# The state's factor from one sum of three angles, and a new set of planner numbers

## The chip, the cores and the metric

One core of a Trainium2 chip runs the program. The metric is the device time of one execution in microseconds, the median of several. Times inside an execution come from the hardware profiler and count from the span's first instruction.

## The reference, cut to what matters

```python
# attention: a recurrence with a complex decay a = a_re + i a_im per (token, row of the state)
mag = np.sqrt(a_re * a_re + a_im * a_im)
scale = np.minimum(mag, 0.999) / (mag + 1e-06)
a_re_n, a_im_n = a_re * scale, a_im * scale
for t in range(S):                                  # B, H, S, D = 4, 8, 768, 48
    new_re = ar * S_re - ai * S_im
    new_im = ar * S_im + ai * S_re
    S_re, S_im = new_re + einsum(k[t], v[t]), new_im
    y[t] = einsum(q[t], S_re)
# then x = y as rows (3072 x 384): experts of 384 tokens each (relu(x @ w1) @ w2),
# and last (x @ w_a) * (x @ w_b) @ w_out
```

## The kernel before

The attention works in chunks of 128 tokens. Its loop index i runs over 12 pairs: six chunks, each with two halves of the batch, so that pair i covers two units (n = 2i and 2i + 1) of 128 tokens by 8 heads by 48. For each pair `gates` makes the logarithm of the decay's size, `e`, and its angle, `th`, per token, on ScalarE (Ln, Exp, Square, Arctan) and VectorE. `sums` sums both over the chunk's tokens, from the middle outwards, by matmuls with constant triangles (`Ws`, `Wt`, L354). The sum of the sizes goes through two exponentials into `ea`; the sum of the angles, in turns, is reduced to within half a turn by VectorE and is then `r` (L389, L391). `turned` takes two sines of `r`: `s2` = 2 sin(pi r) squared (L409, L411), which is 1 - cos, and `sn` = sin(2 pi r) (L410); with them it turns q and k into `nat` (L413 to L422). `unit` transposes `nat` (L519), copies it (`qkT`, L522), makes the scores (L531), masks them (`Ab`, L533), multiplies with v (L559), adds the state's part (L566), and sends the rows out (L572 to L586). `outer` (L542) and `keep` (L549) make the chunk's addition to the state, `xs`.

`factor(i)` runs for i from 2 to 11, ten times. It carries the state from pair i - 2 over to pair i: the state has to be multiplied, per head and row of the state, by a complex factor that spans from the middle of one chunk to the middle of the next. Its angle has three parts: what the earlier chunk sums to behind its middle (row 127 of pair i - 2), the angle `th` of the new chunk's first token, and what the new chunk sums to ahead of its middle (row 0 of pair i). These are single rows of 16 x 48 values; small DMAs on SP's queue bring them into the tile `fw` (16 partitions): L427 from `turned`, L342 from `gates`. Before, the rows were of `s2` and `sn` for the first and third part, and ScalarE took the cosine and the sine of `th` (L450, L452). VectorE then multiplied the three complex numbers out (`one`, L456 to L460; `two`, L464 to L467) and the factor's size in (`three`, L471 to L476). TensorE transposes the result (L482), ScalarE copies it to `pb` (L485), VectorE multiplies `xs` with it (L492, `rta` and `rtb`), one SP DMA pair swaps halves (L496), and VectorE adds to the state `Sb` (L500), which L566 reads.

All of this is recorded as tasks with an engine, an estimated duration, reads and writes. `Plan.order` is a list scheduler over these estimates: at each step it takes the engine on which something can start first, and among the tasks of that engine that could start at that time the one of lowest rank, rank = due x STRETCH - tail + EARLIER[kind], where due is PERIOD x (i + 1) or near it and the kind is the engine's letter with the written tile's name (P TensorE, V VectorE, A ScalarE, S SP, G GpSimd; `Sqk` are the loads of q and k, `Sre` those of a_re, `Vft` VectorE's factor work). A task never starts before its inputs and its buffer are free; nearly every tile has one or two buffers. ScalarE has two tables of functions: "E" with Ln and Exp, "T" with Arctan and Sin. A task whose table isn't loaded gets SWITCH added to its rank, and cannot start before PATIENCE us after it is ready unless the waiting tasks of its table add up to ENOUGH us. The instructions are then issued in that order on each engine's queue, so each queue waits in order. The planner doesn't know POOL's set-up work, which is ahead of it on POOL's queue.

After the attention come the router, which counts tokens per expert, and the experts with their last layer; these are 780 us of mostly TensorE work, written out in another way.

Of the kernel before, what the change touches and what calls it, by code (L numbers as in the profile page):

```python
# [14 lines left out]
AF = mybir.ActivationFunctionType  # L15
OP = mybir.AluOpType
# [5 lines left out]
B, H, S, D = 4, 8, 768, 48  # L22
# [4 lines left out]
LN = math.log  # L27
HALF_PI = math.pi / 2
TB = 12
MAGIC = 1.5 * 2 ** 21  # L30
TURN = 1.5 * 2 ** 23
LIFT = 12.125
PERIOD = 22.0
SWITCH = 13.0
HOP = {"P": 0.22, "V": 0.08, "A": 0.08, "S": 0.08, "G": 0.08}
NPAIR = 2
LANDING = 1.5
SPLIT_PAIRS = 3
EARLIER = {'Acc': 8, 'Aea': 5, 'Ag': -6, 'Aln': -14, 'Apb': -15, 'AqkT': -2, 'Arec': -6, 'As2': 2, 'Asf': -23, 'Asn': 6, 'Ath': 6, 'Axo': 6, 'AyT': 17, 'G-': 1, 'PF': -10, 'PHH': -10, 'PLL': -2, 'PO': -10, 'PS': 13, 'PTT': -1, 'PX': 2, 'PY': 5, 'Sends': 9, 'Sfw': 6, 'Sim': 10, 'Sqk': 11, 'Sre': -1, 'Ssw': 15, 'Sv': -13, 'V-': -5, 'VAb': 3, 'VS': 3, 'Ve': 10, 'Vearly': -1, 'Veb': 2, 'Vft': 21, 'Vg': 4, 'Vlg': -17, 'Vn4': -5, 'Vnat': -7, 'Vr': 4, 'Vrt1': -2, 'Vsetup': -4, 'Vxs': 4}
STRETCH = 0.844334  # L40
LONG = ("LL", "HH")
ENGINES = "PVASG"
SLOW = 1.03
SINGLE = 1
PATIENCE = 9.0
ENOUGH = 8.5
BUFS = {'rho': 2, 'ln': 2, 'g': 2, 'e': 2, 'ea': 2}


# [4 lines left out]
class Plan:  # L54
# [31 lines left out]
    def order(self):  # L86
# [5 lines left out]
        for t in reversed(T):  # L92
            own = [T[u]["tail"] for u in users[t["n"]] if T[u]["due"] == t["due"]]
            t["tail"] = t["dur"] + t["land"] + HOP[t["eng"]] + max(own, default=0.0)
            t["rank"] = t["due"] * STRETCH - t["tail"] + EARLIER.get(t["kind"], 0.0)
        left = [len(t["after"]) for t in T]
# [10 lines left out]
        def places(key):  # L107

            if len(key[0]) == 2:
                if key[0] in LONG:  # L110
                    used = [h for k, h in holds.items() if k[0] in LONG]
                    if len(used) >= SPLIT_PAIRS:
                        return []
# [3 lines left out]
        while any(waiting.values()):  # L117
            best = None
            for e, w in waiting.items():
# [14 lines left out]
                if not ok:  # L134
                    continue
                first = min(ok)[0]
                now = [(T[n]["rank"] + (SWITCH if T[n]["table"] and T[n]["table"] != table else 0.0), n)
                       for at, n in ok if at <= first + 1e-9]
# [50 lines left out]
def attention(tc, q, k, v, a_re, a_im, wg, x_dram, consts, L, guard, router, tail_work=None):  # L189
# [4 lines left out]
    A, V, G, PE = nc.scalar, nc.vector, nc.gpsimd, nc.tensor  # L194
    SP = nc.sync
    NB = NU // 2
    PI = math.pi
    with ExitStack() as st:
# [5 lines left out]
        def many(pool, n, shape, name, dt=F32):  # L204
            return [pool.tile(shape, dt, name=f"{name}{i}") for i in range(n)]

        W1, W2 = 2 * HD, HD
        plan = Plan(many(ps, NPAIR, [128, 2, 512], "pair") + many(ps, 8 - 2 * NPAIR, [128, 512], "bank"))
# [3 lines left out]
        tables = {"E": "natural_log_exp_and_others", "T": "trig_and_small"}  # L212
        A.preload_act_table_set(tables["E"])
        bias = {}
        for nm, x in (("one", 1.0), ("shift", LIFT), ("tiny", LN(2.0e-6)), ("quarter", HALF_PI)):
            bias[nm] = cst.tile([128, 1], F32, name="b_" + nm)
            V.memset(bias[nm], x)

# [34 lines left out]
        ends = cst.tile([2 * H, NB, 2, D], F32, name="ends")  # L253
        fw = many(cst, 4, [2 * H, 8, D], "fw")
# [139 lines left out]
        def turned(i, due):  # L394

            a = dict(due=due)
            c, pair = divmod(i, 2)
            j = i % 2
            (r, kr), (s2, ks2), (sn, ksn), (ea, kea), (eb, keb) = [buf(nm, i) for nm in ("r", "s2", "sn", "ea", "eb")]
            ea, eb = [t.rearrange("p (a r d) -> p a r d", a=2, d=D) for t in (ea, eb)]  # L400
            y = i % len(nat)

            def both(k):
                return [k + (0,), k + (1,)]
            for us in parts(i):
                def K(k, us=us):
                    return [k + (u,) for u in us]
                x, z = cols(us), rows_of(us)
                plan.add("A", took(0.83, us), lambda x=x: A.activation(s2[:, x], r[:, x], AF.Sin, scale=PI), K(kr), K(ks2), table="T", **a)  # L409
                plan.add("A", took(0.83, us), lambda x=x: A.activation(sn[:, x], r[:, x], AF.Sin, scale=2 * PI), K(kr), K(ksn), table="T", **a)  # L410
                plan.add("A", took(0.83, us), lambda x=x: A.activation(s2[:, x], s2[:, x], AF.Square, scale=math.sqrt(2.0)),  # L411
                         K(ks2), K(ks2), **a)
                plan.add("V", took(1.7, us), lambda z=z: V.tensor_mul(eb[:, :, z], ea[:, :, z], ld_qk[j][:, :, z]),  # L413
                         K(kea + (0,)) + K(kea + (1,)) + [("qk", j, 0), ("qk", j, 1)], K(keb), **a)

                def tr(t, z=z):
                    return t.rearrange("p (r d) -> p r d", d=D)[:, z]
                for w in range(2):
                    plan.add("V", took(0.92, us), lambda w=w, z=z, tr=tr: V.scalar_tensor_tensor(
                        nat[y][:, w, z, 0], tr(s2), 1.0, eb[:, w, z], op0=OP.subtract, op1=OP.mult),  # L420
                        K(ks2) + K(keb), K(("nat", y, w, 0)), **a)
                plan.add("V", took(1.78, us), lambda z=z, tr=tr, m=len(us): V.tensor_mul(  # L422
                    nat[y][:, :, z, 1], eb[:, :, z], tr(sn)[:, None].to_broadcast([128, 2, m * H, D])),
                    K(ksn) + K(keb), K(("nat", y, 0, 1)) + K(("nat", y, 1, 1)), **a)

            def row(dst, key, t, reads, at):
                plan.add("S", 0.55, lambda: SP.dma_start(dst, t[at:at + 1].rearrange("p (r d) -> p r d", d=D)),  # L427
                         reads, [key], land=LANDING, **a)
            fa = buf("ea", i)[0].rearrange("p (a x) -> p a x", a=2)
            row(ends[:, i, 0], ("ends", i, 0), fa[:, 0], both(kea + (0,)), 127)  # L430
            row(ends[:, i, 1], ("ends", i, 1), fa[:, 1], both(kea + (1,)), 0)
            if c < NCK - 1:
                w = (i + 2) % 4
                row(fw[w][:, 0], ("fw", w, 0), s2, both(ks2), 127)
                row(fw[w][:, 1], ("fw", w, 1), sn, both(ksn), 127)
            if c:
                w = i % 4
                row(fw[w][:, 2], ("fw", w, 2), s2, both(ks2), 0)
                row(fw[w][:, 3], ("fw", w, 3), sn, both(ksn), 0)

        def factor(i, due):

            a = dict(due=due)
            y = i % 4
            f, w, b = fw[y], ft[0], pb[i % 2]
            kf = [("fw", y, s) for s in range(8)]
            kw = ("ft", 0)
            plan.add("A", 0.22, lambda: A.activation(f[:, 6], f[:, 6], AF.Exp, scale=0.5),
                     [kf[6]], [kf[6]], table="E", **a)
            plan.add("A", 0.22, lambda: A.activation(f[:, 4], f[:, 7], AF.Sin, bias=bias["quarter"][0:16]),  # L450
                     [kf[7]], [kf[4]], table="T", **a)
            plan.add("A", 0.22, lambda: A.activation(f[:, 5], f[:, 7], AF.Sin), [kf[7]], [kf[5]], table="T", **a)  # L452
            sh = [2 * H, 2, 2, D]

            def one():
                V.tensor_scalar(f[:, 0:3:2], f[:, 0:3:2], -1.0, 1.0, op0=OP.mult, op1=OP.add)  # L456
                V.tensor_tensor(w[:, 0:4].rearrange("p (a b) d -> p a b d", a=2), f[:, None, 0:2].to_broadcast(sh),
                                f[:, 2:4, None].to_broadcast(sh), op=OP.mult)
                V.tensor_tensor(w[:, 4], w[:, 0], w[:, 3], op=OP.add)
                V.tensor_tensor(w[:, 5], w[:, 1], w[:, 2], op=OP.subtract)  # L460
            plan.add("V", 0.92, one, kf[0:4], [kw, kf[0], kf[2]], **a)

            def two():
                V.tensor_tensor(w[:, 0:4].rearrange("p (a b) d -> p a b d", a=2), w[:, None, 4:6].to_broadcast(sh),  # L464
                                f[:, 4:6, None].to_broadcast(sh), op=OP.mult)
                V.tensor_tensor(w[:, 6], w[:, 0], w[:, 3], op=OP.subtract)
                V.tensor_tensor(w[:, 7], w[:, 1], w[:, 2], op=OP.add)  # L467
            plan.add("V", 0.66, two, [kw] + kf[4:6], [kw], **a)

            def three():  # L470
                V.scalar_tensor_tensor(w[:, 4], ends[:, i - 2, 0], math.exp(-2 * LIFT), ends[:, i, 1], op0=OP.mult, op1=OP.mult)  # L471
                V.tensor_tensor(w[:, 5], w[:, 4], f[:, 6], op=OP.mult)
                sh2 = [2 * H, 2, D]
                V.tensor_tensor(w[:, 8:10], w[:, 6, None].to_broadcast(sh2), w[:, 5, None].to_broadcast(sh2), op=OP.mult)
                V.tensor_tensor(w[:, 10], w[:, 7], w[:, 5], op=OP.mult)
                V.scalar_tensor_tensor(w[:, 11], w[:, 7], -1.0, w[:, 5], op0=OP.mult, op1=OP.mult)  # L476
            plan.add("V", 0.9, three, [kw, kf[6], ("ends", i - 2, 0), ("ends", i, 1)], [kw], **a)
            kp = ("F", i)

            def turn():  # L480
# [1095 lines left out]
```

## Time and profile before

| | us |
|---|---|
| median of 3 runs | 1072.03 (1070.23 to 1072.71) |
| profiled execution, its time | 1073.87 |
| profiled execution, its span | 1072.3 |
| TensorE busy | 981.7 (92%) |
| VectorE busy | 649.8 (61%) |
| ScalarE busy | 486.9 (45%) |

The attention takes the first 292 us or so, and the change is in it alone. The shares over the whole span say little of it: there the three engines are all nearly full, and it needs the table of stretches. Matmul records overlap and their ends are modelled, so the start-to-start of two groups is a better measure than a group's own time. DMA-issuing instructions are not busy time.

### The profile page before, as it was taken

The page shows a single profiled execution, that of the slowest core. Times are in us where ns is not written, and L with a number is a line of the kernel's source. Part 1 is how long each engine was busy: PE and PEld are TensorE (multiplying, and loading weights), DVE is VectorE, ACT ScalarE, POOL GpSimd, SP SyncE. Part 2 cuts the span into 40 slices and gives each one's busy share as a digit, 9 for nine tenths or more (in the row PEclk, how much of TensorE's full clock was granted, in tenths as well). Part 3 has the DMA queues.
Part 4 walks back from the last instruction along what each step waited for, and adds up shares of the span by engine and source line. Part 5 has one row for each costly group of instructions (what it writes and reads, how often), then busy time and mean ns, then how long its engine had stood idle before and what let it go on. Part 6 is the DMA issues. An engine that isn't in the chain of part 4 may idle for free. (4 is left out here: it accounts for less than half of the span.)

```text
span 1072.3 us, 17244 instructions
## 1 busy us (share of the span) xinstructions
PE 981.7 (92%) x6587; PEld 896.9 (84%) x6587; DVE 649.8 (61%) x1632; ACT 486.9 (45%) x870; POOL 168.1 (16%) x217
## 2 busy tenths in 40 slices
PE   1789999999838996899999999999999999999994
PEld 0477788887727795799999999999999999999994
DVE  3578898998777899844365445546536544333321
ACT  4689889988414443442332332243233234233321
POOL 6000000000022021122121220320212123202001
PEclk9999999999956998799999999999999999999997
DMA  9586667542144454212110210310211112201000
GB/s 169 76 144 128 120 125 130 102 87 63 47 143 132 117 174 151 67 53 82 38 45 26 79 59 1 104 45 15 82 37 45 42 62 71 92 16 45 1 1 25
DMA packets 146618, 81.49 MB, mean 76 GB/s; under 512 B 130400, under 2 KB 132320, under 8 KB 146528
## 3 DMA queue, kind: packets, MB, share of 16 engines
q1 hardware_dynamic: 134304, 40.97, 20.0%
q0 software_dynamic: 12224, 39.34, 11.3%
q8 instruction: 53, 0.87, 0.4%
q14 instruction: 37, 0.30, 0.1%
HBM read 67.65 MB, written 9.44 MB: 72 GB/s over the span
## 5 line engine op out<-in xcount | busy, mean ns | idle before, releaser
L1253 DVE TENSOR_TENSOR g<-mm,a_s 128x384 f32<-128x384 f32 x96 | 53.3, 556 | 153.8 <-PE mm L1220 130.9
L1072 ACT ACTIVATE gh<-g 128x384 fp32r<-128x384 f32 x96 | 50.3, 525 | 160.0 <-DVE g L1253 159.9
L1248 ACT ACTIVATE a_s<-mm 128x384 f32<-128x384 f32 x96 | 47.1, 490 | 155.6 <-PE mm L1220 147.1
L1168 PE MATMUL acc<-woh,gh 128*128 128x384 f32 x288 | 97.2, 343 | 1.0 <-ACT woh L712 1.0
L1121 POOL DMA_INDIRECT raw<-moe_w_in,i x64 | 66.7, 1043 | 197.9 <-DVE w2l L1073 109.6
L1169 PE MATMUL acc<-wol,gh 128*128 128x384 f32 x288 | 97.1, 337 | 0.0
L1170 PE MATMUL acc<-woh,gl 128*128 128x384 f32 x288 | 96.7, 337 | 0.0
L1073 DVE TENSOR_TENSOR gl<-g,gh 128x384 fp32r<-128x384 f32 x96 | 53.5, 558 | 38.6 <-ACT gh L1072 37.6
L1220 PE MATMUL mm<-yh,wbh 128*128 128x384 f32 x288 | 73.1, 352 | 4.0 <-ACT wbh L712 3.6
L1220 PE MATMUL mm<-yh,wah 128*128 128x384 f32 x288 | 72.8, 354 | 3.5 <-ACT wah L712 3.4
L1168 PE MATMUL mm<-xh,w1h 128*128 128x384 f32 x192 | 67.6, 352 | 2.8 <-DVE xl L1073 2.2
L1220 PE MATMUL mm<-yl,wah 128*128 128x384 f32 x288 | 68.7, 342 | 0.0
L1220 PE MATMUL mm<-yh,wal 128*128 128x384 f32 x288 | 68.2, 344 | 0.0
L1220 PE MATMUL mm<-yh,wbl 128*128 128x384 f32 x288 | 67.7, 341 | 0.0
L1169 PE MATMUL mm<-xl,w1h 128*128 128x384 f32 x192 | 66.0, 344 | 1.0 <-DVE xl L1073 1.0
L1220 PE MATMUL mm<-yl,wbh 128*128 128x384 f32 x288 | 66.8, 339 | 0.0
L1169 PE MATMUL acc<-hl,w2h 128*128 128x384 f32 x192 | 65.1, 339 | 1.7 <-DVE hl L1195 1.7
L1170 PE MATMUL mm<-xh,w1l 128*128 128x384 f32 x192 | 65.6, 342 | 0.0
L1168 PE MATMUL acc<-hh,w2h 128*128 128x384 f32 x192 | 65.2, 350 | 0.0
L1170 PE MATMUL acc<-hh,w2l 128*128 128x384 f32 x192 | 64.6, 336 | 0.0
L1107 POOL DMA_INDIRECT raw<-moe_w_in,i x24 | 24.7, 1030 | 234.3 <-DVE left L984 168.7
L1072 ACT ACTIVATE w1h<-raw 128x384 fp32r<-128x384 f32 x64 | 32.7, 522 | 58.3 <-PE mm L1169 54.0
(288 smaller groups left out, 2375.2 us busy)
## 6 DMA issues: line engine op xcount, KB each, us to landing
vb<-v_in SPq DMA_DIRECT2D x12, 384.0 KB, 4.4
ld_qk<-q_in SPq DMA_DIRECT2D x12, 384.0 KB, 4.1
ld_qk<-k_in SPq DMA_DIRECT2D x12, 384.0 KB, 6.0
x_rows<-xo POOLq DMA_DIRECT2D x24, 192.0 KB, 2.2
stage<-moe_w_a_in SPq DMA_DIRECT2D x12, 384.0 KB, 3.2
stage<-moe_w_b_in SPq DMA_DIRECT2D x12, 384.0 KB, 3.2
stage<-moe_w_out_in SPq DMA_DIRECT2D x12, 384.0 KB, 3.1
ld_re<-a_re_in SPq DMA_DIRECT2D x11, 384.0 KB, 6.0
```

Source lines behind the costliest of these rows:

```text
L1072: a = A.activation(hi, src, AF.Copy)
L1073: return a, V.tensor_tensor(lo_, src, hi, op=OP.subtract)
L1107: G.indirect_dma_start(out=raw[:, j], out_offset=None, in_=w1r, in_offset=bass.IndirectOffsetOnAxis(ap=i1[:, j:j + 1], axis=0))
L1121: G.indirect_dma_start(out=raw, out_offset=None, in_=w2r, in_offset=bass.IndirectOffsetOnAxis(ap=i2[:, f:f + 1], axis=0))
L1168: PE.matmul(p, lh, rh, start=first, stop=False)
L1169: PE.matmul(p, lh, rl, start=False, stop=False)
L1170: PE.matmul(p, ll, rh, start=False, stop=last)
L1220: PE.matmul(p, a[:, j, c], b[:, j], start=(n == 0), stop=(n == 8))
L1248: A.activation(a_s, pa, AF.Copy)
L1253: V.tensor_tensor(g, pb, a_s, op=OP.mult)
```

## The change

The rows that are sent for the factor are now of `r` itself: two per pair where four were. `factor` adds the three angles in turns (`angle`), brings the sum back to within half a turn, and ScalarE takes two sines of that sum. The size is multiplied out by itself (`size`), and `three` makes 1 - cos from the first sine and multiplies the size in. The constant `quarter` goes. All numbers of the planner are new: SWITCH, STRETCH, PATIENCE, ENOUGH, SPLIT_PAIRS and the table EARLIER.

```diff
-SWITCH = 13.0
+SWITCH = 188
-SPLIT_PAIRS = 3
-EARLIER = {..., 'Sqk': 11, 'Sre': -1, 'Sv': -13, 'Vft': 21, 'Vsetup': -4, ...}
-STRETCH = 0.844334
+SPLIT_PAIRS = 2
+EARLIER = {..., 'Sqk': 469, 'Sre': 63, 'Sv': 13, 'Vft': -342, 'Vsetup': 53, ...}
+STRETCH = 4.0
-PATIENCE = 9.0
-ENOUGH = 8.5
+PATIENCE = 3
+ENOUGH = 62.5
...
             if c < NCK - 1:
                 w = (i + 2) % 4
-                row(fw[w][:, 0], ("fw", w, 0), s2, both(ks2), 127)
-                row(fw[w][:, 1], ("fw", w, 1), sn, both(ksn), 127)
+                row(fw[w][:, 0], ("fw", w, 0), r, both(kr), 127)
             if c:
                 w = i % 4
-                row(fw[w][:, 2], ("fw", w, 2), s2, both(ks2), 0)
-                row(fw[w][:, 3], ("fw", w, 3), sn, both(ksn), 0)
+                row(fw[w][:, 1], ("fw", w, 1), r, both(kr), 0)
...
-            plan.add("A", 0.22, lambda: A.activation(f[:, 4], f[:, 7], AF.Sin, bias=bias["quarter"][0:16]),
-                     [kf[7]], [kf[4]], table="T", **a)
-            plan.add("A", 0.22, lambda: A.activation(f[:, 5], f[:, 7], AF.Sin), [kf[7]], [kf[5]], table="T", **a)
...
-            plan.add("V", 0.92, one, kf[0:4], [kw, kf[0], kf[2]], **a)
...
-            plan.add("V", 0.66, two, [kw] + kf[4:6], [kw], **a)
+            def angle():
+                V.scalar_tensor_tensor(f[:, 0], f[:, 7], 0.5 / PI, f[:, 0], op0=OP.mult, op1=OP.add)
+                V.tensor_tensor(f[:, 0], f[:, 0], f[:, 1], op=OP.subtract)
+                V.tensor_scalar(f[:, 1], f[:, 0], TURN, TURN, op0=OP.add, op1=OP.subtract)
+                V.tensor_tensor(f[:, 0], f[:, 0], f[:, 1], op=OP.subtract)
+            plan.add("V", 0.86, angle, [kf[0], kf[1], kf[7]], [kf[0], kf[1]], **a)
+            plan.add("A", 0.22, lambda: A.activation(f[:, 3], f[:, 0], AF.Sin, scale=PI), [kf[0]], [kf[3]], table="T", **a)
+            plan.add("A", 0.22, lambda: A.activation(f[:, 2], f[:, 0], AF.Sin, scale=2 * PI), [kf[0]], [kf[2]], table="T", **a)
+            def size():
+                V.scalar_tensor_tensor(w[:, 4], ends[:, i - 2, 0], -math.exp(-2 * LIFT), ends[:, i, 1], op0=OP.mult, op1=OP.mult)
+                V.tensor_tensor(w[:, 5], w[:, 4], f[:, 6], op=OP.mult)
+            plan.add("V", 0.43, size, [kf[6], ("ends", i - 2, 0), ("ends", i, 1)], [kw], **a)
             def three():
-                V.scalar_tensor_tensor(w[:, 4], ends[:, i - 2, 0], math.exp(-2 * LIFT), ends[:, i, 1], op0=OP.mult, op1=OP.mult)
-                V.tensor_tensor(w[:, 5], w[:, 4], f[:, 6], op=OP.mult)
-                sh2 = [2 * H, 2, D]
-                V.tensor_tensor(w[:, 8:10], w[:, 6, None].to_broadcast(sh2), w[:, 5, None].to_broadcast(sh2), op=OP.mult)
-                V.tensor_tensor(w[:, 10], w[:, 7], w[:, 5], op=OP.mult)
-                V.scalar_tensor_tensor(w[:, 11], w[:, 7], -1.0, w[:, 5], op0=OP.mult, op1=OP.mult)
-            plan.add("V", 0.9, three, [kw, kf[6], ("ends", i - 2, 0), ("ends", i, 1)], [kw], **a)
+                V.scalar_tensor_tensor(f[:, 3], f[:, 3], 2.0, f[:, 3], op0=OP.mult, op1=OP.mult)
+                V.scalar_tensor_tensor(w[:, 8:10], f[:, 3, None].to_broadcast(sh), 1.0, w[:, 5, None].to_broadcast(sh),
+                                       op0=OP.subtract, op1=OP.mult)
+                V.scalar_tensor_tensor(w[:, 10], f[:, 2], -1.0, w[:, 5], op0=OP.mult, op1=OP.mult)
+                V.tensor_tensor(w[:, 11], f[:, 2], w[:, 5], op=OP.mult)
+            plan.add("V", 0.85, three, [kw, kf[2], kf[3]], [kw, kf[3]], **a)
```

## Rows read from the trace of the kernel before

**Rows 1.** Table of stretches: start:end, length, busy per engine (x instructions), clock, DMA, GB/s

```profile
20.00:50.00 30.00, 22.18 (x73) 12.86 (x74) 14.78 (x22) 20.51 (x34) 0.00 (x0) 1.00 0.66 89
50.00:70.00 20.00, 14.63 (x106) 10.67 (x106) 15.20 (x19) 18.39 (x26) 0.60 (x1) 0.95 1.15 185
70.00:260.00 190.00, 188.22 (x1716) 155.60 (x1716) 168.30 (x314) 170.45 (x246) 9.74 (x18) 1.00 0.56 106
260.00:292.00 32.00, 29.87 (x308) 26.68 (x306) 23.82 (x65) 18.09 (x28) 2.16 (x4) 1.00 0.22 58
...
340.00:1072.30 732.30, 703.28 (x4181) 670.31 (x4179) 386.65 (x1058) 240.88 (x503) 126.64 (x125) 0.98 0.19 59
```

**Rows 2.** Timeline of TensorE: start, us, engine, line, tiles, count [idle before <-releaser]

```profile
46.00 1.84 PE L531 MATMUL bank<-qkT 96*128 96x128 f32 x8
...
67.89 2.74 PE L354 MATMUL pair<-th,Wt 128*128 128x384 f32 x4 [3.28 <-ACT th L324]
...
188.77 1.16 PE L531 MATMUL bank<-qkT 96*128 96x128 f32 x8
...
191.88 1.46 PE L354 MATMUL pair<-th,Wt 128*128 128x384 f32 x4
```

**Rows 3.** Groups of instructions in the attention: count | busy us, mean ns | idle before

```profile
L611 ACT ACT_TABLE_LOAD x23 | 29.5, 1283 | 0.4
...
L457 DVE TENSOR_TENSOR ft<-fw 16x192 f32<-16x192 f32 x10 | 3.5, 346 | 0.3
...
L450 ACT ACTIVATE fw<-fw,b_quarter 16x48 f32<-16x48 f32 x10 | 3.3, 334 | 0.1
L474 DVE TENSOR_TENSOR ft<-ft 16x96 f32<-16x96 f32 x10 | 2.5, 246 | 0.3
L452 ACT ACTIVATE fw<-fw 16x48 f32<-16x48 f32 x10 | 2.2, 225 | 0.0
...
L476 DVE SCALAR_TENSOR_TENSOR ft<-ft 16x48 f32<-16x48 f32 x10 | 1.9, 190 | 0.0
```

**Rows 4.** Timeline of ScalarE in the ramp: the two table loads around a long stretch

```profile
37.45 1.28 ACT L611 ACT_TABLE_LOAD   x1
...
62.81 1.28 ACT L611 ACT_TABLE_LOAD   x1
```

**Rows 5.** Timeline of ScalarE in the body: two loads of the T table

```profile
162.56 1.28 ACT L611 ACT_TABLE_LOAD   x1
163.85 0.34 ACT L450 ACTIVATE fw<-fw,b_quarter 16x48 f32<-16x48 f32 x1
...
183.96 1.28 ACT L611 ACT_TABLE_LOAD   x1
```

**Rows 6.** Timeline of VectorE: r complete, a factor's first work, a state's addition

```profile
39.87 0.96 DVE L391 TENSOR_TENSOR r<-pair,r 128x768 f32<-128x768 f32 x1
...
153.68 0.94 DVE L391 TENSOR_TENSOR r<-pair,r 128x768 f32<-128x768 f32 x1
...
174.43 0.19 DVE L456 TENSOR_SCALAR fw<-fw 16x96 f32<-16x96 f32 x1
...
186.97 0.56 DVE L500 TENSOR_TENSOR Sb<-rta,sw 96x384 f32<-96x384 f32 x1 [0.52 <-DMA sw<-rtb]
...
275.50 0.19 DVE L456 TENSOR_SCALAR fw<-fw 16x96 f32<-16x96 f32 x1
```

**Rows 7.** DMA issues in the attention: count, KB each, median us to landing

```profile
fw<-s SPq DMA_DIRECT2D x20, 3.0 KB, 3.2
```

**Rows 8.** Timelines of SP and VectorE at the start

```profile
13.28 2.56 SPq L311 DMA_DIRECT2D ld_qk<-k_in  x1
14.70 0.18 DVE L741 TENSOR_SCALAR iot<-iot 128x32 f32<-128x32 f32 x1 [11.69 <-POOL iot L739]
...
35.65 0.95 DVE L413 TENSOR_TENSOR eb<-ea,ld_qk 128x768 f32<-128x768 f32 x1
```

**Rows 9.** Timeline of TensorE at the end of the attention

```profile
290.51 1.14 PE L579 MATMUL bank<-iw,yT 128*128 128x104 f32 x8 [0.69 <-ACT yT L572]
```

More of the change, by code (lines that the diff above doesn't have):

```diff
@@ L37 @@
 LANDING = 1.5
-SPLIT_PAIRS = 3
-EARLIER = {'Acc': 8, 'Aea': 5, 'Ag': -6, 'Aln': -14, 'Apb': -15, 'AqkT': -2, 'Arec': -6, 'As2': 2, 'Asf': -23, 'Asn': 6, 'Ath': 6, 'Axo': 6, 'AyT': 17, 'G-': 1, 'PF': -10, 'PHH': -10, 'PLL': -2, 'PO': -10, 'PS': 13, 'PTT': -1, 'PX': 2, 'PY': 5, 'Sends': 9, 'Sfw': 6, 'Sim': 10, 'Sqk': 11, 'Sre': -1, 'Ssw': 15, 'Sv': -13, 'V-': -5, 'VAb': 3, 'VS': 3, 'Ve': 10, 'Vearly': -1, 'Veb': 2, 'Vft': 21, 'Vg': 4, 'Vlg': -17, 'Vn4': -5, 'Vnat': -7, 'Vr': 4, 'Vrt1': -2, 'Vsetup': -4, 'Vxs': 4}
-STRETCH = 0.844334
+SPLIT_PAIRS = 2
+EARLIER = {'Acc': -177, 'Ae': -3, 'Aea': -11, 'Afw': -57, 'Ag': 28, 'Aln': 30, 'Apb': -119, 'AqkT': -253, 'Arec': -16, 'As2': 131, 'Asf': 19, 'Asn': -16, 'Ath': -97, 'Axo': 237, 'AyT': -211, 'G-': 32, 'PF': -244, 'PHH': -125, 'PLL': -214, 'PO': 188, 'PS': 151, 'PTT': -114, 'PX': -44, 'PY': -68, 'Sends': 56, 'Sfw': -162, 'Sim': 79, 'Sqk': 469, 'Sre': 63, 'Ssw': 133, 'Sv': 13, 'V-': 161, 'VAb': 148, 'VS': 81, 'Ve': -169, 'Vearly': 92, 'Veb': 209, 'Vft': -342, 'Vfw': -121, 'Vg': -306, 'Vlg': 22, 'Vn4': -325, 'Vnat': 55, 'Vr': 198, 'Vrho': -317, 'Vrt0': 427, 'Vrt1': 251, 'Vsetup': 53, 'Vxs': -466}
+STRETCH = 4.0
 LONG = ("LL", "HH")
@@ L214, in attention @@
         bias = {}
-        for nm, x in (("one", 1.0), ("shift", LIFT), ("tiny", LN(2.0e-6)), ("quarter", HALF_PI)):
+        for nm, x in (("one", 1.0), ("shift", LIFT), ("tiny", LN(2.0e-6))):
             bias[nm] = cst.tile([128, 1], F32, name="b_" + nm)
@@ L449, in factor @@
                      [kf[6]], [kf[6]], table="E", **a)
-            plan.add("A", 0.22, lambda: A.activation(f[:, 4], f[:, 7], AF.Sin, bias=bias["quarter"][0:16]),
-                     [kf[7]], [kf[4]], table="T", **a)
-            plan.add("A", 0.22, lambda: A.activation(f[:, 5], f[:, 7], AF.Sin), [kf[7]], [kf[5]], table="T", **a)
[L453 to L460, printed above, removed]
@@ L461, in factor @@
-            plan.add("V", 0.92, one, kf[0:4], [kw, kf[0], kf[2]], **a)
[L463 to L467, printed above, removed]
-            plan.add("V", 0.66, two, [kw] + kf[4:6], [kw], **a)
@@ L477, in factor @@
-            plan.add("V", 0.9, three, [kw, kf[6], ("ends", i - 2, 0), ("ends", i, 1)], [kw], **a)
+            sh = [2 * H, 2, D]
+            def angle():
[3 more added lines that the diff above has]
+                V.tensor_tensor(f[:, 0], f[:, 0], f[:, 1], op=OP.subtract)
```

## The prediction

> **What bounds the kernel now.** I read the table of stretches first [rows 1]. The readers should see three regimes. From 340 us to the end TensorE is 96% busy on expert layers that the diff does not touch: they start later or earlier with the attention and cost the same. From 70 to 260 us, the body of the attention, TensorE is busy 188.22 of 190 us: it idles 1.78 us, while VectorE idles 190 - 168.30 = 21.7 and ScalarE 190 - 170.45 = 19.55. So the body is bound by TensorE, whose work the change leaves alone. Only the two ends have slack on TensorE: 7.82 us idle in 20 to 50, 5.37 in 50 to 70, and 2.13 in 260 to 292, where the last units drain.
>
> Second, the timeline of TensorE [rows 2]. Its longest wait after the first matmul is 3.28 us at 67.89, for the arctangent of the third pair; the four matmuls behind it take 2.74 us where the same four take 1.46 in the body. That place costs 3.28 + 1.28 = 4.6 us. At 46.00 eight score matmuls still take 1.84 us against 1.16 later, so the early matmuls are slow as well as patchy, although the clock column reads 1.00 there.
>
> Third, ScalarE's table loads [rows 4, 5]. In the body a pair of loads recurs every 183.96 - 162.56 = 21.4 us, one block of sines and arctangent per i. In the ramp the block ends by the load at 37.45 and the next begins at 62.81: 25 us without sines, though the second pair's r is complete at 39.87 + 0.96 = 40.8 [rows 6]. That long run is what makes the arctangent, and so TensorE, late at 67.89.
>
> **The change part by part.** The profiled execution has a span of 1072.3 us and a time of 1073.87; the median of the runs is 1072.03. I add to the span and carry the difference over to the median.
>
> VectorE, per factor: twelve instructions go. Two are 192 wide at 0.346, one 96 wide on a broadcast at 0.246, nine small at 0.190 [rows 3]: 0.69 + 0.25 + 1.71 = 2.65 us. Ten come: nine 48 wide at 0.190 and one 96 wide broadcast at 0.246: 1.96 us. The saving is 0.69 us, times ten factors 6.9 us. None of it is on the path in the body: it only adds to 21.7 us of idle VectorE. At the drain the last factor's VectorE run starts at 275.50 [rows 6] and TensorE idles 2.13 us in that whole stretch [rows 1], so at most the 0.69 once. If the cover were gone, TensorE no longer being the bound, the whole 6.9 us would show; I keep that as an end.
>
> ScalarE, per factor: one exponential and two sines before and after. The sine with a bias operand takes 0.334, the one without 0.225 [rows 3]; both are now without: 0.11 x 10 = 1.1 us, into idle time, so nothing.
>
> SP: of the four rows per state (s2 and sn, 127 and 0) two remain (r). 20 DMAs fewer. SP is no bound; what waits behind those rows gets out earlier. Zero.
>
> The order of the chain changes. Before, the row DMAs left after the sines, and the first of the factor's VectorE work ran at 174.43; the state was added at 186.97 [rows 6], 12.5 us later. Now the rows leave when r is ready: 153.68 + 0.94 = 154.6. They land a median of 3.2 us after issue [rows 7], the angle takes four small instructions, 0.76, so the sines can go at about 159, an estimate from these rows, well ahead of the block at 162.56. The cover is some 4 us. If it goes, angle waits in VectorE's queue for its DMA, and behind it the next i's g, rho and e wait, for which ScalarE's exponentials and then TensorE wait; a sine that misses its block costs a further pair of loads. The state can be ready about ten us earlier, but nothing in the body waits for it: price nothing, gain nothing.
>
> The plan. Every task's rank is due x STRETCH - tail + EARLIER, and STRETCH goes from 0.84 to 4 with offsets of hundreds: by the kinds' offsets more than by due times. The list scheduler still issues anything that is startable, so a kind runs ahead only as far as its one or two buffers let it. In the body I therefore expect the same TensorE bound: the idle there can shrink by 1.78 at most. PATIENCE 9 to 3 lets a task of the other table start 3 us after it is ready, where 9 us were asked before unless 8.5 us of such work had gathered. That bears on the 25 us run in the ramp. The new penalty SWITCH of 188 pulls the other way, but only among tasks that could start at the same moment, and in the ramp ScalarE often has none. I take it that the block comes earlier, and that half of the 4.6 us goes: half, because the loads and the arctangent remain in the queue, and what is late next is VectorE's nat chain. Ends: nothing back, or all 4.6.
>
> The start. EARLIER of the q and k loads goes from 11 to 469; for i = 0 the rank is 12 x 4 + 469 = 517, against 46 x 4 + 63 = 247 for a_re of the third pair, so SP may load the third pair ahead of q and k. Before, the first k was issued at 13.28 for 2.56 us and first used at 35.65 [rows 8]: 35.65 - 15.84 = 19.8 us of cover. Four such loads of about 2.1 us are 8.4; one of them must wait for rho, which runs only after VectorE's wait for POOL at 14.70 [rows 8]. It stays covered, barely: zero, with up to 5 us lost if q and k come behind two such waits. VectorE's 11.69 us wait itself stays: those setup tasks are startable at time zero under either set of ranks.
>
> The drain: TensorE waits 0.69 us for the last yT [rows 9], one of the waits in 2.13 us. I take 1.2 of the 2.13: the last factor is ready earlier by its 0.69 and by rows sent before the sines.
>
> Sum: 2.3 + 1.2 = 3.5 us. Span 1068.8, median 1072.03 - 3.5 = 1068.5.
>
> **The rivals.** A, no change: TensorE's bound holds everywhere and the new ranks only move idle time from one place of the ramp to another. For it: 188.22 of 190 us. Against it: 5.37 + 2.13 us are open. Time 1072.0, within 2.1 us.
>
> B, slower: the sines, which now need a DMA and four VectorE instructions first, miss the block and bring a second pair of loads per i. A pair costs 2 x 1.283 = 2.57 us [rows 3], ScalarE idles 19.55 x 21.4 / 190 = 2.2 us per i. So it decides when nearly every i has a second pair: 0.4 us over, nine times, 3.6, and a ramp with one more wait like that at 67.89 up to 4.6. Time 1072 + 3.6 = 1075.6; with the ramp 1080. Against it: SWITCH and the cover of some 4 us.
>
> The Trainium skill ("ScalarE: Activation LUTs", What ACT_TABLE_LOAD costs) gives 2.66 us per switch, the load and a drain; by it the pair is 5.3 us and B becomes 9 x 3.1 = 28 us, 1100. The trace doesn't show the drain: the sine starts at 163.85, right at the end of the load [rows 5].
>
> C, much faster: the ramp is really repaired. All of 4.6 us at 67.89, the other 2.1 us of idle in 50 to 70, 1.8 in the body and 2.1 at the end: 10.6 us, 1061.4. If TensorE is also filled earlier, part of the 7.82 us before 50 and of the slow matmuls comes on top. For it: the idle time is there. Against it: the ramp is a chain of latencies, and its first link, POOL, isn't in the plan.
>
> **How the numbers follow.** A measurement of this kernel can tell about 0.2%, 2.1 us, from no change. Forecast (2.1 to 6 us faster) 0.38; C (over 6 us) 0.14; A 0.25; B or a ramp that is worse by one more wait 0.23. Faster 0.52, same 0.25, slower 0.23. The range takes in C's 1061 and B's 1075.6, rounded to 1076; what is left out is C with an earlier TensorE, and B with the ramp.
>
> **What would show it.** Step by step: ten VectorE instructions per factor with 1.96 us; two r rows where four rows went; 23 table loads in the attention as before [rows 3] (over 40 would be B); TensorE idle in the body still under 2 us per 190, with the same 21 us between blocks; the wait at the third pair's arctangent shorter; the last output matmuls of the attention before 290.51 [rows 9]. I am wrong if the body's TensorE idle grows (the new ranks break the bound), if the first matmuls of the ramp wait for q and k, or if the ramp's gain goes to another wait.

## The result: 8 us slower, and the profile after

The changed kernel takes 1079.62 us (median of four, 1078.65 to 1080.97) where the kernel before takes 1071.54 beside it: a ratio of 1.0077, 95% interval 1.0063 to 1.0091. The forecast was 1068.5 with a range of 1061 to 1076; sign and range are both missed. The profiled execution has a span of 1078.6 us and a time of 1080.24, so its span is 6.3 us longer than that of before.

The same stretches as [rows 1], with the same columns (start:end, length, busy time of TensorE, its weight loads, VectorE, ScalarE, GpSimd, then granted clock, DMA share, GB/s), now of the changed kernel:

```profile
20.00:50.00 30.00, 18.08 (x52) 9.49 (x53) 18.47 (x27) 22.73 (x38) 0.00 (x0) 0.77 0.91 139
50.00:70.00 20.00, 19.01 (x142) 15.04 (x140) 11.10 (x15) 17.64 (x24) 0.60 (x1) 0.92 0.40 57
70.00:260.00 190.00, 179.89 (x1591) 148.65 (x1591) 159.74 (x305) 163.59 (x239) 8.65 (x16) 0.97 0.60 110
260.00:292.00 32.00, 32.00 (x324) 28.84 (x324) 24.90 (x48) 19.16 (x28) 2.70 (x5) 0.98 0.21 55
```

Third row first. In the body TensorE idles 190 - 179.89 = 10.11 us, against 1.78 before: 8.3 us more, about the size of the loss. The two needn't be equal, as a slow matmul counts as busy time. VectorE, which the change was to relieve, idles more too: 30.3 us against 21.7. So neither engine is the bound there any longer; both wait for something else.

VectorE's waits from 20 to 300 us say for what (engine, tile and line waited for: us in total, times, longest):

```profile
DVE Ab L528 <- PE bank L526: 13.8, 17, 2.3
DVE ft L462 <- DMA ends<-ea: 13.8, 5, 4.8
...
DVE fw L453 <- DMA fw<-r: 3.0, 3, 2.0
...
DVE r L389 <- DMA fw<-r: 1.9, 1, 1.9
```

The first is ordinary traffic between TensorE and VectorE. The second is new: L462 is the first instruction of `size`, and it waits 13.8 us in five of the ten factors for the rows of `ends`. Before, the same multiplication stood at the head of `three` (L471 there) and no wait for these rows is in its trace. The other two are the waits for `r` rows that the new angle brings: `angle` itself (3.0), and a tile `r` that can't be written again until its row is sent (1.9).

The longest of the five, on VectorE's timeline (start, us, line, tiles, [idle before it <- what ended it]):

```profile
157.95 0.54 DVE L544 TENSOR_TENSOR xs<-bank,Sb 96x384 f32<-96x384 f32 x1
163.24 0.20 DVE L462 SCALAR_TENSOR_TENSOR ft<-ends 16x48 f32<-16x48 f32 x1 [4.76 <-DMA ends<-ea]
163.47 0.20 DVE L463 TENSOR_TENSOR ft<-ft,fw 16x48 f32<-16x48 f32 x1
163.60 0.94 DVE L331 TENSOR_TENSOR rho<-ld_im,rec 128x768 f32<-128x768 f32 x1
164.47 1.74 DVE L413 TENSOR_TENSOR eb<-ea,ld_qk 128x1536 f32<-128x1536 f32 x1
166.14 0.17 DVE L576 TENSOR_REDUCE L<-bank 128x8 f32<-128x32 f32 x1
166.24 0.94 DVE L370 TENSOR_SCALAR n<-pair 128x768 bf16<-128x768 f32 x1
```

Two instructions of 0.20 us hold up `rho`, `eb` and `n` of the next pair, which are 128 partitions wide and on which ScalarE and TensorE depend. TensorE over the same time:

```profile
162.50 1.45 PE L354 MATMUL pair<-th,Wt 128*128 128x384 f32 x4
167.23 0.80 PE L354 MATMUL pair<-n,eye_minus 128*128 128x384 bf16 x2 [3.28 <-DVE n L370]
...
169.89 5.49 PE L526 MATMUL bank<-qkT 96*128 96x128 f32 x24
...
290.06 2.86 PE L526 MATMUL bank<-qkT 96*128 96x128 f32 x24
```

It idles 3.28 us for `n`. What follows is slow as well: 24 score matmuls take 5.49 us, where 24 of the same shape take 2.86 at 290.06. The granted clock in the two stretches around it (columns as above):

```profile
160.00:170.00 10.00, 6.72 (x34) 5.02 (x32) 6.36 (x12) 5.42 (x9) 0.54 (x1) 0.80 0.63 109
170.00:180.00 10.00, 10.00 (x77) 8.86 (x78) 6.52 (x10) 7.21 (x11) 0.54 (x1) 0.69 0.50 111
```

0.69 lies between the two levels of 2.4 and 1.2 GHz; a group that takes 5.49 / 2.86 = 1.9 times as long is nearly all at the lower one. So behind this wait of 3.28 us come up to 2.6 us more in slow matmuls.

Why the rows come late stands on SP's timeline:

```profile
154.82 0.54 SPq L427 DMA_DIRECT2D ends<-ea  x1
155.46 0.53 SPq L308 DMA_DIRECT2D ld_re<-a_re_in  x1
156.08 1.16 SPq L313 DMA_DIRECT2D vb<-v_in  x1
157.33 1.74 SPq L427 DMA_DIRECT2D ends<-ea  x1
```

The second `ends` row, 3 KB, is issued at 157.33, behind two loads of 384 KB. VectorE reaches `size` at 158.5 and gets the row at 163.2, 5.9 us after the issue. Over the attention the `ends` rows take 1.6 us at least, 2.5 in the median and 6.6 at most from issue to landing; the planner reckons with LANDING = 1.5. In the kernel before, a pair's two rows on SP's timeline, and their reader on VectorE's:

```profile
164.40 1.17 SPq L427 DMA_DIRECT2D ends<-ea  x2
```
```profile
177.62 0.19 DVE L471 SCALAR_TENSOR_TENSOR ft<-ends 16x48 f32<-16x48 f32 x1
```

There the reader came 13 us after the issue; now VectorE is at it 1.2 us after.

The attention's last output matmuls, which answer to [rows 9]:

```profile
297.73 2.03 PE L574 MATMUL bank<-iw,yT 128*128 128x104 f32 x16
```

They end at 299.76 against 290.51 + 1.14 = 291.65: the whole loss has arisen by then.

### The profile page after: what moved, and what is told of

Same layout as the page of the kernel before. It is cut to its first block, busy times and chain, and to the rows that moved or that the text cites. A ratio compares the mean times of both kernels' runs of the same rounds, so it can differ in the third digit from the quotient of the medians.

```text
span 1078.6 us, 17175 instructions
## 1 busy us (share of the span) xinstructions
PE 980.5 (91%) x6587; PEld 896.9 (83%) x6587; DVE 644.3 (60%) x1611; ACT 484.6 (45%) x870; POOL 168.2 (16%) x217
```

## The experiments

The theory: the loss is the early wait of `size`. Its rivals: the new planner numbers as such (another order of everything), the `r` rows that `angle` waits for, and the price of the rows on SP's queue. One table of all runs, each compared with the kernel before on the same chip (medians of before there: 1070.07 to 1071.54). "Idle" is 190 less TensorE's busy time in 70 to 260; "ends" is VectorE's wait in the factor for the `ends` rows, "angles" that for the rows of the angles (of `r`, or of `s2` and `sn` in the factor of before), both over the attention; "last" is the end of the attention's last output matmuls. The last four columns are of each kernel's profiled execution.

| kernel | median us | ratio, 95% | idle | ends | angles | last |
|---|---|---|---|---|---|---|
| before | 1071.54 | 1 | 1.78 | 0 | 0 | 291.65 |
| after | 1079.62 | 1.0077 (1.0063 to 1.0091) | 10.11 | 13.8 | 3.0 | 299.76 |
| e1 changed factor, old numbers | 1110.89 | 1.0361 (1.0323 to 1.0400) | 24.53 | 6.5 | 16.4 | 333.94 |
| e2 old factor, new numbers | 1085.0 | 1.0146 (1.0112 to 1.0181) | 9.88 | 0 | 4.8 | 303.12 |
| e3 `size` late | 1072.1 | 1.0011 (0.9994 to 1.0027) | 5.37 | 0.2 | 4.9 | 291.78 |
| e4 ends rows from GpSimd | 1071.19 | 1.0003 (0.9982 to 1.0024) | 5.35 | 3.5 | 6.0 | 293.36 |
| e5 `size` late, r rows from GpSimd | 1070.3 | 0.9986 (0.9968 to 1.0005) | 4.50 | 0 | 3.8 | 288.06 |
| e6 before, setup first | 1093.96 | 1.0191 (1.0155 to 1.0227) | 17.40 | 0 | 0.3 | 313.15 |
| e7 e5 with setup first | 1065.8 | 0.9946 (0.9928 to 0.9965) | 3.25 | 0 | 5.5 | 287.29 |
| e8 e1, all these rows from GpSimd | 1109.17 | 1.0372 (1.0325 to 1.0419) | 17.23 | 0 | 10.8 | 321.34 |
| e9 planner told that ends rows land late | 1106.41 | 1.0334 (1.0304 to 1.0365) | 21.71 | 0 | 10.3 | 322.70 |
| e10 e3 with the wait put back | 1078.97 | 1.0076 (1.0050 to 1.0101) | 7.63 | 12.7 | 2.7 | 297.07 |

### The two halves of the change, apart

e1 keeps the changed factor and takes the planner's numbers of before; the factor's new kind gets the offset that the old one had.

```diff
-SWITCH = 188
+SWITCH = 13.0
-EARLIER = {..., 'Vft': -342, ...}
-STRETCH = 4.0
+EARLIER = {..., 'Vft': 21, 'Vfw': 21, ...}
+STRETCH = 0.844334
-PATIENCE = 3
+PATIENCE = 9.0
...
```

> The changed factor (rows of r, angle, size, three) under the planner numbers of before; angle gets the offset 21 that the old factor tasks had. Theory 1 (the wait of size for its ends rows, put early in VectorE's queue by the new numbers, is the loss): VectorE no longer waits for ends rows, TensorE's idle time in the body is back to about 2 us per 190, and the time is that of before within 2 us, 1070 to 1073. Rival (the new factor itself costs it, since its sines now wait for a DMA and for VectorE): it stays near 1079, with waits of ScalarE for angle or of VectorE for the r rows.

e2 keeps the factor of before and takes the new numbers: SWITCH, SPLIT_PAIRS, EARLIER, STRETCH, PATIENCE and ENOUGH, nothing else.

> The factor of before (one, two, three) under the new planner numbers. Theory 1: three waits for its ends rows only after one and two, so the wait is short, and the time is 1071 to 1074. Rival (the new ranks put the matmuls or the table loads in a worse order, whatever the factor does): about 1079 or more, without a wait of VectorE for ends rows over 2 us.

e1 is 3.6% slower, e2 1.5%: each half alone is worse than both together, so the losses can't be shared out by adding halves. Theory 1 missed in both. In e1 `size` still waits for its rows, 6.5 us in two factors, so its early place isn't the work of the new numbers alone. In e2 no task of the factor waits for `ends` rows (one read outside it, at 254, waits 3.7 us, more than the rival allowed), and the time is 1085 all the same, the rival's. Rows of e1, VectorE's waits from 20 to 345 us, then the body in the columns of the stretches:

```profile
DVE fw L453 <- DMA fw<-r: 16.4, 8, 3.6
...
DVE ft L462 <- DMA ends<-ea: 6.5, 2, 5.0
```
```profile
70.00:260.00 190.00, 165.47 (x1359) 135.25 (x1358) 137.56 (x258) 139.80 (x202) 7.58 (x14) 0.91 0.47 91
```

Here `angle` stands in VectorE's queue before its rows have landed, eight times. That looked like the cause. e8 tests it by sending these rows from GpSimd's queue, which takes them out from behind the loads:

```diff
-                plan.add("S", 0.55, lambda: SP.dma_start(dst, ...
+                Q = G if key[0] in ('fw', 'ends') else SP
+                plan.add("S", 0.55, lambda: Q.dma_start(dst, ...
```

> The changed factor under the numbers of before, as in e1, with r rows and ends rows issued from POOL. If e1's 40 us are VectorE's 20.7 us of waits for rows and what they set off: 1075 to 1090. If they are the order that numbers fitted to other tasks give: the waits go, and the time stays over 1100.

The wait for `ends` goes altogether, that for `r` falls from 16.4 to 10.8, TensorE's idle time in the body falls by 7.3 us, and the median moves by 1.7, inside its spread. So the 12 us of waits that went were worth next to nothing; the 10.8 that are left weren't tested. That the order which the old numbers make out of the new tasks is a bad one as a whole is the likelier reading, but it isn't shown, and which tasks it places badly stays open.

### Taking the wait of size away, two ways

e3 moves the two instructions of `size` to the head of `three`, where they were before. The planner still sees a task at the old place, which issues nothing, so the order of all else is that of the changed kernel.

```diff
-            plan.add("V", 0.43, size, [kf[6], ("ends", i - 2, 0), ("ends", i, 1)], [kw], **a)
+            plan.add("V", 0.43, lambda: None, [kf[6], ("ends", i - 2, 0), ("ends", i, 1)], [kw], **a)
             def three():
+                size()
```

> The changed kernel in its own issue order, with the two instructions of size moved behind: they run at the head of three, the place that the plan gave them is left empty. Theory 1: VectorE's 13.8 us of waits for ends rows fall under 2 us, TensorE's idle time from 70 to 260 falls from 10.1 to 3 or 4 us, and the time falls by 6 to 9 us to 1071 to 1074. Rival (the ranks' order as a whole): the waits go, others take their place, and the time stays above 1077.

e4 leaves `size` early and issues the `ends` rows from GpSimd's queue (the edit of e8 with `key[0] == "ends"`).

> The changed kernel with the ends rows issued from POOL's queue in place of SP's, everything else as it was. Theory 1a (a row issued on SP lands late because 384 KB loads are queued ahead of it on the same queue): landing falls from up to 6.6 us to about 2.5, VectorE's wait for ends rows falls by half or more, the time to 1072 to 1076. Theory 1b (the row is sent late, by the exponential that makes it, and any queue lands it too late): the waits and the time stay within 2 us.

Both come back to the kernel before: 1.0011 and 1.0003. The same place in e3, first VectorE, then TensorE:

```profile
160.95 0.96 DVE L370 TENSOR_SCALAR n<-pair 128x768 bf16<-128x768 f32 x1 [1.19 <-PE pair L354]
161.92 0.20 DVE L462 SCALAR_TENSOR_TENSOR ft<-ends 16x48 f32<-16x48 f32 x1
```
```profile
161.97 0.49 PE L354 MATMUL pair<-n,eye_minus 128*128 128x384 bf16 x2
...
164.86 4.50 PE L527 MATMUL bank<-qkT 96*128 96x128 f32 x24
```

`n` now runs ahead of `size`, waits for TensorE instead of making it wait, and TensorE goes on at 161.97 without the 3.28 us. The repair isn't whole: a later wait of 1.15 us, for the factor's transpose, stands before the 24 score matmuls, which still take 4.50 us, and the body idles 5.37 us where 3 or 4 were expected. In e4 `size` is still ahead; its waits over the attention, one factor's own, and the first of the two stretches:

```profile
DVE ft L463 <- DMA ends<-ea: 3.5, 4, 1.5
```
```profile
158.63 0.20 DVE L463 SCALAR_TENSOR_TENSOR ft<-ends 16x48 f32<-16x48 f32 x1 [0.66 <-DMA ends<-ea]
```
```profile
160.00:170.00 10.00, 10.00 (x77) 7.92 (x77) 8.52 (x15) 9.64 (x17) 1.11 (x2) 1.00 0.94 172
```

GpSimd issues the second row at 155.00, 0.3 us after ScalarE has written `ea`, where SP did so 2.1 us after; so it is now ahead of the second load, which SP issues at 155.27. The row is there 3.6 us after its issue instead of 5.9. TensorE is busy all of 160 to 170, at a granted clock of 1.00 instead of 0.80, and the 24 score matmuls take 2.94 us. The Trainium skill ("DMA: Bandwidth & Descriptors", Queues, rings and completion order) has each transfer engine take turns between the queues that have work for it, while one queue's own work is taken in order. That agrees with 3.6 against 5.9 us; the runs don't separate it from the earlier issue.

### Putting the wait back alone

e3 and e4 also change when `size` itself is done. e10 is e3 with a single product of one column of the two rows in the old place of `size`, whose result nobody reads: it brings back the wait, and no work.

```diff
+            def look():
+                V.tensor_tensor(w[:, 0, 0:1], ends[:, i - 2, 0, 0:1], ends[:, i, 1, 0:1], op=OP.mult)
-            plan.add("V", 0.43, lambda: None, [kf[6], ("ends", i - 2, 0), ("ends", i, 1)], [kw], **a)
+            plan.add("V", 0.43, look, [kf[6], ("ends", i - 2, 0), ("ends", i, 1)], [kw], **a)
```

> As e3 (size at the head of three), with one multiplication of a single element of the two ends rows put where the plan had size: the wait without the work. Theory 1 (the wait itself, in VectorE's queue, is the loss): VectorE waits about 13 us for ends rows again and the time goes back to 1077 to 1081. Rival (what helped in e3 is that work was moved, not that a wait went): it stays at 1071 to 1073.

The total of its waits, one of them on VectorE's timeline, and TensorE behind it:

```profile
DVE ft L461 <- DMA ends<-ea: 12.7, 5, 4.5
```
```profile
163.46 0.15 DVE L461 TENSOR_TENSOR ft<-ends 16x1 f32<-16x1 f32 x1 [4.49 <-DMA ends<-ea]
```
```profile
167.16 0.49 PE L354 MATMUL pair<-n,eye_minus 128*128 128x384 bf16 x2 [2.78 <-DVE n L370]
...
168.68 5.49 PE L530 MATMUL bank<-qkT 96*128 96x128 f32 x24
```

The ratio is 1.0076, that of the changed kernel (1.0077), and the pattern is back: five waits, TensorE late for `n`, 24 score matmuls in 5.49 us. Ten products of 0.15 us add 6.9 us to e3 (1078.97 - 1072.1; against the before of each batch, 8.9 and 1.3).

e3, the changed kernel and e10 issue their work in one order, so the same matmul can be followed through all three. This is the start of a pair's first `n` matmul (L354, `pair<-n,eye_minus`), and last the end of the attention's output matmuls, in us:

| pair | e3 | after | after less e3 | e10 |
|---|---|---|---|---|
| third | 63.61 | 63.66 | 0.05 | 60.71 |
| fifth | 99.31 | 101.43 | 2.12 | 101.56 |
| seventh | 143.90 | 145.72 | 1.82 | 146.14 |
| eighth | 161.97 | 167.23 | 5.26 | 167.16 |
| ninth | 186.52 | 192.94 | 6.42 | 190.99 |
| eleventh | 230.96 | 237.38 | 6.42 | 235.44 |
| end | 291.78 | 299.76 | 7.98 | 297.07 |

In the changed kernel `size` gets its rows at 76.37, 136.96, 163.24, 188.37 and 253.49, after waits of 2.51, 1.09, 4.76, 1.98 and 3.46 us. The lag grows around the first and the last three of them and hardly elsewhere; the wait of 1.09 costs nothing. So the lag of 8.0 us lies at four waits. In this execution of e10 the ramp ran 2.9 us quicker than in e3; from there to the end it loses 8.2 us. Together with e3 and e4 this shows that the wait is the loss, and not some other place of the order, nor the amount of VectorE's work. Which of the two put `size` early, its being a task of its own or the new numbers, isn't separated.

### What is left once the wait is gone

e5 is e3 with the `r` rows sent from GpSimd's queue (the edit of e8 with `key[0] in ('fw',)`).

> The changed kernel with size at the head of three, and the r rows issued from POOL's queue. With size late alone VectorE still waited 6.8 us for r rows, 1.9 of it at the third pair's r in the ramp. Theory 1 (every small row that VectorE reads soon after it is sent costs what it lands late): these waits fall under 2 us and the time falls by 1 to 4 us against size late alone, to 1068 to 1071. Rival (those waits lie beside TensorE's own work): the waits go and the time stays at 1071 to 1073.

Its ratio is 0.9986, e3's 1.0011; the intervals overlap, so the second remedy is worth 2 or 3 us or nothing. It didn't do what was expected of it: the wait for these rows is only a little shorter, 3.8 us against 4.9, and that of the tile `r` for its sending is 2.0 against 1.9.

e9 repairs the planner's view instead of the kernel: it is told that `ends` rows land 4.5 us after their issue.

```diff
-                         reads, [key], land=LANDING, **a)
+                         reads, [key], land=4.5 if key[0] == "ends" else LANDING, **a)
```

> The changed kernel, with the planner told that an ends row lands 4.5 us after its issue and not 1.5. If the planner's estimate is the root and nothing else hangs on it: VectorE's waits for ends rows go and the time is that of e3, 1070 to 1074. If the numbers hold only for the task list and durations with which they came (as e1, e2, e6 and e8 suggest): the waits go, the order changes elsewhere too, and the time is 1080 to 1110.

It removes the wait for `ends`, as it should, and costs 3.3%: the idle time of the body is 21.71 us. One true number among fitted ones gives another order, with 25 table loads instead of 23 and 10.3 us of waits for `r` rows.

The prediction named VectorE's wait for GpSimd at the start [rows 8] as one that stays. e6 takes the kernel before and has the router's setup issued ahead of the late memsets on GpSimd and of the plan on VectorE:

```diff
+        for f in router.setup:
+            f()
         late_setup()
...
-        for f in router.setup:
-            plan.add("V", 0.2, f, ["setup"], ["setup"], due=PERIOD * 3)
```

> The kernel before, with the router's set-up issued ahead of the attention's own set-up on POOL and ahead of the plan on VectorE. The planner doesn't know that VectorE's set-up waits 11.69 us for POOL. If that wait sets the start (first step of the ramp), the first matmul comes 7 to 10 us earlier and the time falls by 5 to 9 us, to 1062 to 1066. Rival (the ramp is bound by the loads of q, k and the third pair, which come from one queue at 2 us each): the first matmul is early and the time falls by under 3 us.

Neither expectation holds. The first matmul comes 3 us earlier (17.62 instead of 20.66), and the kernel is 1.9% slower: with another list of tasks the order is another one (21 table loads instead of 23), and the body idles 17.40 us. e7 puts the same edit on e5:

> The changed kernel with size late, r rows from POOL, and the router's set-up first. If the three effects add: the time of e5 less what e6 gains, 1060 to 1066. If the new numbers' ramp is bound by its q and k loads (they are issued after the third pair's a_re and a_im), the gain of the set-up is 4 us or more smaller here than in e6.

```profile
17.61 1.62 PE L356 MATMUL pair<-e,Ws 128*128 128x384 f32 x2 [17.61 <-DVE e L329]
```
```profile
70.00:260.00 190.00, 186.75 (x1703) 154.93 (x1702) 164.92 (x316) 166.69 (x244) 19.00 (x37) 0.99 0.55 106
```

Here too the order is another one than in e5 (the work between ScalarE's table loads differs), but not a worse one: first matmul at 17.61, 3.25 us idle in the body, 1065.8 us, ratio 0.9946. The time is in the range that was expected, though e6 gave no gain that could have been added. It beats both kernels, by 5 to 6 us the one before and by some 14 the changed one. How much of the 4.5 us between e5 and e7 is the earlier start and how much the new order isn't separated.

## Why the prediction was wrong

**What bounds the kernel now.** The reading of before stands: 1.78 us idle in the body. The step that failed is what I made of it: "I therefore expect the same TensorE bound: the idle there can shrink by 1.78 at most". A busy share tells how much there is to gain, not that it is kept. TensorE was full because VectorE, idle for 21.7 us, delivered in time; a change in VectorE's order can take that away without touching TensorE, and 4.8 us of waiting in the wrong place is enough. The idle time grew by 8.3.

**The added wait.** I named `angle`, with "some 4 us" of cover and the queue behind it, and that description fits what happened, to another task. `angle` itself waits 3.0 us in all. I counted `size` only as two of ten instructions, though the diff gives it a task of its own, with the rows of `ends` among its reads, and its kind `Vft` goes from 21 to -342. The question that I asked of `angle` wasn't asked of `size`: what has to have landed, when is it issued, and how soon can the list scheduler now put the reader behind it? The landing row that I had [rows 7] was of other 3 KB rows and twice the planner's 1.5. It held the warning: any row whose reader is placed by that 1.5 can be a wait of some us. I drew the estimate from it for `angle` alone.

**The counts.** VectorE's work is as forecast: the ten instructions' means, 0.194 and 0.196 for `size`, 0.190, 0.196, 0.176 and 0.196 for `angle`, 0.188, 0.246, 0.190 and 0.189 for `three`, add up to 1.96 us. The sines take 0.232 and 0.225. "None of it is on the path" holds as well: with the wait removed, e3 stands within 0.3% of before.

**The ramp.** Forecast: half of 4.6 us, 2.3. In 50 to 70 us TensorE's idle time fell from 5.37 to 0.99, more than that. The block of sines and arctangent came at 53.92 instead of 62.81, which is the mechanism as forecast, and the place that was priced was repaired whole, without a wait:

```profile
65.54 1.56 PE L354 MATMUL pair<-th,Wt 128*128 128x384 f32 x4
```

But in 20 to 50 us the idle time rose from 7.82 to 11.92. Over both it is 12.91 against 13.19, and the third pair's first `n` matmul starts at 63.66 against 63.36: nothing. The matmuls also stay slow for longer: before, four of L354 take 1.45 us from 47.84 on; in the changed kernel eight transposes still take 1.94 at 49.74 (1.04 at 55.59). The clock column of the two kernels can't be compared here: the first clock record lies at 47.6 us in the trace of before and at 29.5 in that of the changed kernel, and time without a record counts as 1.00. So the 1.00 at which the prediction wondered [rows 2] says nothing. The term was mis-sized, 2.3 for nothing: this is what rival A said of the ramp ("only move idle time from one place of the ramp to another").

**The start and the drain.** q and k came later (the first k at 16.06, the second at 32.12), and no wait for them shows: zero, as forecast. In 260 to 292 TensorE's idle time went from 2.13 to 0, but the work there is now what was done earlier before, so the 1.2 us that were forecast aren't a gain at the end.

**The rivals.** B had the sign with the wrong mechanism. Its second pair of table loads didn't come:

```profile
L606 ACT ACT_TABLE_LOAD x23 | 29.5, 1283 | 0.4
```

23 loads, as in [rows 3]. With the ramp on top it stood at 1080, which is the time that was measured, but that is luck: neither the 3.6 us of loads nor the 4.6 us of a worse ramp came. C's gain is nowhere. Without the wait, A is what the change amounts to: 1.0011, interval 0.9994 to 1.0027.

**What I said would show it.** "I am wrong if the body's TensorE idle grows (the new ranks break the bound)": that is what the table of stretches showed first. The last case, "if the ramp's gain goes to another wait", came as well. The first was named, but had no price and no chance of its own.

**What stays open.** Four times another pairing of numbers and tasks was slower, by 14 to 40 us (e1, e2, e6, e9); once, in e7, it was faster. Which placement makes each of those orders slow or fast isn't shown.

## What to carry to other kernels

Where a change splits an instruction off from a task, or gives its kind another rank, ask of each piece what must have landed for it and how long that takes in the trace: in an in-order queue a 0.2 us instruction that waits 4.8 us holds up everything behind it. An engine that is 99% busy is full only as long as its suppliers keep their order, so price the loss of that as a rival. A planner's numbers may hold for one list of tasks alone, as four of five other pairings here were slower: undo the suspected placement with the order kept, as in e3 and e10, before changing the numbers.

## What the hardware showed that I had not expected

A 3 KB row behind two loads of 384 KB took 5.9 us from issue to landing; such rows need 1.6 us at best.

In e6, small instructions of VectorE took some six times as long beside GpSimd's memsets. VectorE, then GpSimd:

```profile
8.49 1.77 DVE L230 TENSOR_SCALAR eye_plus<-ident 128x128 bf16<-128x128 f32 x1
...
10.38 4.58 DVE L768 COPY fold<-ident 32x32 f32<-32x32 f32 x4
```
```profile
8.74 1.45 POOL L265 MEMSET Sb<- 128x512 f32 x3
10.24 3.68 POOL L267 MEMSET qkT<- 32x2048 f32 x2
```

The first takes 0.30 us in the kernel before, at 2.35. The four copies take 4.58 us, against 0.72 in the kernel before, and end at 14.96, when GpSimd's last memset there ends (14.93). The Trainium skill ("SBUF — State Buffer", Who interferes with whom) says that VectorE's copies and tensor-scalar operations in their fast modes share a pair of ports with GpSimd, and that the engine which comes second is held up for the whole instruction. These rows agree with it, though no view tells whether these instructions ran in such a mode; no run here puts the same instructions beside an idle GpSimd in the same place.
